# Rounding constants in two row groups, a later Silu, and earlier exponentials in an S4 and MLP block

## The chip, the cores and the metric

The kernel runs on one core of one Trainium2 chip. The core has five engines that run side by side: TensorE (PE) multiplies matrices into PSUM, VectorE (DVE) and ScalarE (ACT) work on elements, GpSimd (POOL) and SyncE (SP) here mostly issue transfers (DMA). Each works through its own instructions in order and waits on semaphores for the others. The metric is the device time of one execution in microseconds (us); less is better.

## The reference

The input is a sequence `x` of 2048 rows with 512 channels. A condition vector `c` is passed through Silu and multiplied by `w_mod`, which gives six rows of modulation: shift, scale and gate for each of two halves.

```python
mod = (_silu(c) @ w_mod).reshape(c.shape[0], 6, 1, -1)
h = _layernorm(x) * (1 + ca) + sa
x = x + ga * _A_ref(h, ...)      # S4: a long convolution along the sequence
h = _layernorm(x) * (1 + cb) + sb
x = x + gb * _B_ref(h, ...)      # dense 512 -> 1792, mish, dense 1792 -> 512
```

The convolution kernel of each channel is `K[d, l] = Re sum_n C[d,n] dB[d,n] exp(dt[d] A[d,n] l)` with 128 complex states `n` per channel and 2048 positions `l`; the reference convolves by FFT.

## The kernel before

The 512 channels are four blocks of 128; a block is worked in eight chunks of 16 channels, so there are 32 chunks `k`, with `b, c = divmod(k, 8)`. For each chunk the powers `exp(dt A l)` are made from a product of a fine and a coarse table, each of a magnitude (exponential) and an angle (sine and cosine).

*The parameters of block 0* come first and at the top of the program: `params(0, stage)` (lines 443 to 505) takes logarithm, exponential and an arc tangent (stages 1 and "atan", ScalarE) with VectorE's arithmetic between them, and leaves them split in `pk`. `load_s` (507) for block 0 spreads `pk` over partitions with matmuls (`psel`) and ScalarE copies (`s`). `coarse_mm` and `coarse` (533, 541) are the matmuls into `pco` and the exponentials of them into `co` and `cf`, four groups to a block.

*The angle of a chunk* is `s_ang` (554). It accumulates eight data matmuls into `pang` (two PSUM banks, one buffer), half with `ac`, half with `nac = -ac`. Between the two halves a large constant is added and subtracted again, which rounds what is there to a whole number, so that the second half leaves the negative fraction of a turn. The constant is made by matmuls of ones (`oneb`) against a column (`rnd`), 512 wide: in block 0 with all 128 rows and the constant divided by 128, four matmuls for a chunk; in blocks 1 to 3 with 32 rows and the constant divided by 32, the two banks in different row groups (rows 0 to 31 and 64 to 95), again four. `s_sin` (583) takes the absolute value and two sines from `pang` into `ec`, `s_mag` and `s_comb` (590, 599) multiply in the magnitudes on VectorE, `s_kgen` (610) contracts over the states on TensorE into `pkg`, and `s_ks`, `s_ka`, `s_tm` (622 to 640) bring the result into `gk`.

*The signal's side:* layer norm of the rows (`stats`, `norm_scales`, `norm`), a first transform (`ua`, with ScalarE's copies `us` and their stores to `ud` in DRAM), the modulation (`mod_load`, `mod_mm` and what follows; it reads `sc`, the output of Silu), then per step `gl`, `ubu`, `ug`, `ubk`, `prod`, `t1`, `yt`, `invb`, `z`. The shift's row passes through `srt`, `sra`, `srv` once, before the first `ubu`. After the convolution come a second layer norm and the MLP, from about 350 us on.

*Order.* V, A and T are wrappers (293) that keep the instructions of VectorE, ScalarE and TensorE in the order in which the program issues them. For the first chunks that order is written out by hand (lines 905 to 1106). For the rest `_plan` (57) makes it, a list scheduler: each operation has an engine, a cost in ns (`NS`), a due time (`LEAD` or `AT`, in chunks), what it depends on, and the PSUM banks that it takes from a ring of six and that another operation frees. An engine that is free takes the ready operation with the earliest due time; one whose banks are not yet free is passed over. A switch of ScalarE's table between sine (table "S") and exponential ("E") costs `SWITCH`, and once in "E" the planner holds sines back until the block's exponentials are done. `vt` (coarse matmuls, three banks each) and `va` (their exponentials) are numbered by group: `vt` and `va` 4 to 7 are those of block 1. `p0` to `p5` and `pa` are the stages of `params` for blocks 1 to 3, `ls` is `load_s`. An activation whose function is not in the loaded table set gets a load in front of it; `tables(...)` places one.

## Time and profile before

| | |
|---|---|
| median of 3 runs | 688.12 us (684.78 to 692.02) |
| the profiled execution | 687.09 us |
| its span, first to last instruction | 685.3 us |
| mean granted TensorE clock | 0.970 |
| TensorE busy | 626.3 us (91%) |
| VectorE busy | 475.4 us (69%) |
| ScalarE busy | 403.7 us (59%) |

The profile is of one execution. In a line of the order of time stand the start in us, the busy time in us, the engine, the line of the program, the operation, what it writes and reads with sizes, and how many instructions were merged (x); in brackets how long the engine was idle ahead of it, and what ended the wait. Nearly all instructions are issued through a helper, so their line is L301; they are told apart by their tiles. PEld is TensorE's loading of weights, which runs beside its matmuls. A line of waits has who waited for whom: us in total, times, and the longest.

### The profile page before, as it was taken

To read this page: it belongs to the slowest core of one execution; us is meant where nothing else is said; L and a number is where in the kernel's file an instruction comes from. 1 tells how busy PE (TensorE), PEld (TensorE's weight loads), DVE (VectorE), ACT (ScalarE), POOL (GpSimd) and SP (SyncE) were. 2 spreads that over 40 slices of the span, in tenths; PEclk is the share of its full clock that TensorE was granted. 3 is DMA by queue.
4 is the path that set the end of the run, shared out by engine and by line. 5 is a ranking of instruction groups with operands and counts; after the bars stand their busy time and mean duration, and the time that the engine had idled before them with its cause. 6 is when DMAs were issued, how large, how long until landed. Compare 5 with 4: busy or idle time off the path is not lost.

```text
span 685.3 us, 16585 instructions
## 1 busy us (share of the span) xinstructions
PE 626.3 (91%) x6740; PEld 506.1 (74%) x6746; DVE 475.4 (69%) x903; ACT 403.7 (59%) x707; POOL 101.5 (15%) x212
## 2 busy tenths in 40 slices
PE   0658878999989999999999999999999999999997
PEld 0424556778867777777875888789889898998996
DVE  5997974999689995997676799586337723653233
ACT  3478778877889769876653664453345334534231
POOL 2002705063406240000100000000000001000100
PEclk9979978799999999999999999999999999999999
DMA  9938978353457466555898987666334552273232
GB/s 253 213 151 247 239 182 218 101 144 76 103 161 188 128 182 174 153 146 160 248 269 235 316 284 241 229 176 200 116 93 141 167 154 94 93 222 116 93 93 62
DMA packets 108220, 117.55 MB, mean 172 GB/s; under 512 B 12904, under 2 KB 84976, under 8 KB 106992
## 3 DMA queue, kind: packets, MB, share of 16 engines
q1 hardware_dynamic: 93296, 85.62, 43.9%
q0 software_dynamic: 14464, 30.36, 15.6%
q8 instruction: 53, 0.87, 0.6%
q10 hardware_dynamic: 384, 0.52, 0.3%
q14 instruction: 23, 0.19, 0.1%
HBM read 81.85 MB, written 32.51 MB: 167 GB/s over the span
## 4 chain that ended last, share of the span: by engine, by line
PE 67%; DMA 12%; ACT 9%; DVE 7%; issue 3%; SPq 2%; ACTq 0%; DVEq 0%
PE pr L301 25%; PE pp L301 9%; PE pkg L301 7%; PE pang L301 6%; PE pub L301 5%; PE pib L301 4%; ACT ec L301 3%; PE pkb L301 3%; PE pt L301 2%; DMA xr<-in_A_u 2%; DMA wm<-in_w_mod 2%; DMA ud<-us 2%; PE pia L301 2%; DMA w1s<-in_B_w 2%; DMA w2s<-in_B_w 2%
## 5 line engine op out<-in xcount | busy, mean ns | idle before, releaser
L301 PE MATMUL pr<-hh,w 128*128 128x256 f32 (+1 forms) x420 | 78.2, 327 | 0.5 <-ACT hh L301 0.5
L301 ACT ACTIVATE ec<-pang 128x1024 f32<-128x1024 f32 x64 | 62.2, 1025 | 23.3 <-PE pang L301 23.3
L301 PEld LDWEIGHTS pr<-hh,w 128*128 128x128 f32 x420 | 66.6, 188 | 12.7 <-ACT hh L301 1.9
L301 DVE TENSOR_TENSOR mh<-x,pr 128x256 f32<-128x256 f32 x63 | 26.4, 419 | 65.2 <-PE pr L301 64.9
L301 PE MATMUL pp<-w,mah 128*128 128x512 f32 x224 | 70.5, 396 | 0.0
L301 PE MATMUL pr<-w,mah 128*128 128x512 f32 x224 | 70.0, 394 | 0.0
L301 DVE TENSOR_TENSOR ec<-ec,m 128x1024 f32<-128x1024 f32 x64 | 61.2, 957 | 9.9 <-ACT ec L301 7.8
L1259 POOL DMA_DIRECT2D w<-w2d x42 | 22.2, 529 | 300.9 <-PE pp L301 201.7
L301 ACT ACTIVATE mh<-mh,b 128x256 f32<-128x256 f32 x63 | 32.1, 510 | 52.4 <-DVE mh L301 52.1
L528 POOL DMA_DIRECT2D s<-pk x96 | 47.5, 501 | 61.9 <-PE pang L301 53.9
L301 ACT ACTIVATE mh<-pr,b 128x256 f32<-128x256 f32 (+1 forms) x35 | 19.4, 558 | 62.5 <-PE pr L301 62.5
L301 DVE TENSOR_TENSOR q<-pkb,ug 128x1024 f32<-128x1024 f32 x32 | 39.1, 1221 | 17.0 <-PE pkb L301 16.7
L301 DVE TENSOR_TENSOR mal<-mh,mah 128x512 fp32r<-128x512 f32 x56 | 38.5, 688 | 14.5 <-ACT mah L301 14.3
L301 DVE TENSOR_TENSOR m<-cf 128x1024 f32<-128x1024 f32 x32 | 39.0, 1218 | 13.7 <-ACT cf L301 13.7
L301 PE MATMUL pp<-w,mal 128*128 128x512 f32 x112 | 43.9, 392 | 0.0
L301 PE MATMUL pr<-w,mal 128*128 128x512 f32 x112 | 43.9, 392 | 0.0
L301 ACT ACTIVATE ug<-pub,gd 128x512 f32<-128x512 f32 x64 | 34.0, 590 | 14.9 <-PE pub L301 14.9
L301 PEld LDWEIGHTS pp<-w,mah 128*128 128x128 f32 x224 | 38.4, 189 | 4.9
L301 DVE TENSOR_TENSOR x<-x,pr 128x256 f32<-128x256 f32 x42 | 17.6, 420 | 34.4 <-PE pr L301 34.4
L301 PEld LDWEIGHTS pkg<-ec 128*32 128x32 f32 x2048 | 34.7, 115 | 8.0 <-issue 1.8
L526 POOL DMA_DIRECT2D s<-pk x48 | 23.8, 501 | 112.7 <-ACT ks L301 60.2
L301 PE MATMUL pkg<-ec 128*32 128x64 f32 x2048 | 40.1, 232 | 0.0
(172 smaller groups left out, 1421.6 us busy)
## 6 DMA issues: line engine op xcount, KB each, us to landing
w<-w2d POOLq DMA_DIRECT2D x42, 512.0 KB, 3.6
ud<-us SPq DMA_DIRECT2D x64, 128.0 KB, 2.7
gu<-ud SPq DMA_DIRECT2D x32, 256.0 KB, 3.0
zd<-z SPq DMA_DIRECT2D x32, 256.0 KB, 3.8
zt<-zd SPq DMA_DIRECT2D x32, 256.0 KB, 4.8
w2d<-w SPq DMA_DIRECT2D x14, 512.0 KB, 4.2
xf<-x2d SPq DMA_DIRECT2D x16, 256.0 KB, 5.0
x2d<-xp SPq DMA_DIRECT2D x14, 256.0 KB, 3.2
```

Source lines behind the costliest of these rows:

```text
L301: ins = f(*a, **kw)
L526: nc.gpsimd.dma_start(S3[b, i][q, :], pk[32 * i:32 * i + 32, 8 + k, :])
L528: nc.gpsimd.dma_start(S12[b, g][64 * e + 16 * k:64 * e + 16 * k + 16].rearrange("p h n -> p (h n)"), pk[d, k + 4 * e, :])
L1259: nc.gpsimd.dma_start(t, w2d[f])
```

## The change

Three edits. Silu of the condition moves from the head of ScalarE's program to just behind the arc tangent of block 0. The rounding in block 0 takes the form that blocks 1 to 3 have: 32 rows, the two banks in two row groups; for that the loop over the two halves of the data becomes the outer one. In the planner's tables the first coarse matmuls of block 1 (`v1`) get the due time -14 instead of -4.01, which holds for their exponentials too, and those matmuls depend on the sine of chunk 7 instead of chunk 8 (`- (b == 1)`); the exponentials still depend on the sine of chunk 8. The planner's cost of a `us` copy goes from 540 to 580.

```diff
-      "sc": 2600, "nr": 450, "ua": 1150, "us": 540, "we": 240, "na": 490, "lf": 60, "sr": 400}
+      "sc": 2600, "nr": 450, "ua": 1150, "us": 580, "we": 240, "na": 490, "lf": 60, "sr": 400}
...
-      "p0": -20.55, "p1": -7.87, "v1": -4.01, "v2": -4.01, "v3": -4.01, "vn": 1.22, "e1": 0, "e2": 0, "e3": 0,
+      "p0": -20.55, "p1": -7.87, "v1": -14, "v2": -4.01, "v3": -4.01, "vn": 1.22, "e1": 0, "e2": 0, "e3": 0,
...
-            op(("vt", 4 * b + n), "T", k + AT[f"v{b}"] + n * AT["vn"], [("ls", 2 * b, PART), ("sin", k + AT[f"e{b}"])], 3)
+            op(("vt", 4 * b + n), "T", k + AT[f"v{b}"] + n * AT["vn"], [("ls", 2 * b, PART), ("sin", k + AT[f"e{b}"] - (b == 1))], 3)
...
+    def rounding(p):
+        for z in range(2):
+            for e in range(2):
+                r = slice(64 * e, 64 * e + 32)
+                T.matmul(p[:, e, :], oneb[r].to_broadcast([32, P]), rnd[r, 2 + z:3 + z].to_broadcast([32, 512]),
+                         start=False, stop=False, skip_group_check=True)
+
...
-            for e in range(2):
-                for w in (ac, nac):
+            for w in (ac, nac):
+                for e in range(2):
                     for q in range(2):
...
-                    for z in range(2) if w is ac else ():
-                        T.matmul(p[:, e, :], oneb.to_broadcast([P, P]), rnd[:, z:z + 1].to_broadcast([P, 512]),
-                                 start=False, stop=False, skip_group_check=True)
+                if w is ac:
+                    rounding(p)
...
-            for z in range(2) if w is ah else ():
-                for e in range(2):
-                    r = slice(64 * e, 64 * e + 32)
-                    T.matmul(p[:, e, :], oneb[r].to_broadcast([32, P]), rnd[r, 2 + z:3 + z].to_broadcast([32, 512]),
-                             start=False, stop=False, skip_group_check=True)
+            if w is ah:
+                rounding(p)
...
-    act(sc, cT, AF.Silu)
     nc.sync.dma_start(hl, io["hl"])
...
     params(0, "atan")
+    act(sc, cT, AF.Silu)
     params(0, 2.6)
```

## The prediction

> **What bounds the kernel now.** I read the page first, then busy time by stage, then the waits of the engines up to 200 us, then the order of time in the three places that the diff touches. The first fence is the page's busy line and the busy time by stage (PE, PEld, DVE, ACT, POOL; then granted clock, DMA share, GB/s).

> ```profile
> PE 626.3 (91%) x6740; PEld 506.1 (74%) x6746; DVE 475.4 (69%) x903; ACT 403.7 (59%) x707; POOL 101.5 (15%) x212
> ...
> 0.00:25.00 25.00, 2.11 (x8) 1.43 (x8) 16.77 (x68) 6.31 (x10) 3.78 (x18) 1.00 0.99 245
> 25.00:50.00 25.00, 16.24 (x67) 10.90 (x68) 23.38 (x74) 18.31 (x31) 0.00 (x0) 0.80 0.64 178
> 50.00:75.00 25.00, 20.46 (x284) 10.25 (x281) 19.90 (x30) 20.99 (x37) 9.93 (x21) 0.86 0.83 224
> 100.00:125.00 25.00, 21.14 (x406) 16.07 (x400) 14.79 (x37) 18.43 (x32) 8.96 (x18) 0.77 0.79 216
> 125.00:150.00 25.00, 23.69 (x357) 17.97 (x357) 24.31 (x38) 21.41 (x38) 6.67 (x14) 0.93 0.38 104
> 150.00:175.00 25.00, 25.00 (x521) 20.27 (x523) 24.60 (x27) 16.96 (x32) 9.40 (x20) 1.00 0.36 90
> ```

> From 150 us on TensorE is busy in all of its 25.00 us at clock 1.00, with VectorE at 24.60 beside it: from there nothing that the diff touches can move the end, except by letting that stretch begin earlier. Before it TensorE is not full and its clock falls to 0.77. All three edits lie ahead of 135 us. So the question is how many microseconds each takes off the start of the full stretch.

> The waits of ScalarE up to 200 us name the two that the diff aims at:

> ```profile
> ACT ec L301 <- PE pang L301: 13.3, 10, 3.0
> ACT sc L301 <- DMA cT<-in_c: 10.3, 1, 10.3
> ```

> **Part 1, Silu behind the arc tangent.** The order of time at the start:

> ```profile
> 0.73 1.28 ACT L301 ACT_TABLE_LOAD   x1 [0.73 <-PEq L1521]
> ...
> 10.94 0.43 DVE L301 TENSOR_TENSOR raw<-raw 128x256 f32<-128x256 f32 x1
> 12.36 0.21 ACT L301 ACTIVATE sc<-cT 128x4 f32<-128x4 f32 x1 [10.34 <-DMA cT<-in_c]
> 12.58 1.28 ACT L301 ACT_TABLE_LOAD   x1
> ...
> 14.43 1.04 ACT L301 ACTIVATE early<-early 128x1024 fp32r<-128x1024 f32 x1
> 14.55 0.29 DVE L301 TENSOR_TENSOR raw<-raw 128x128 f32<-128x128 f32 x1 [3.19 <-ACT raw L301]
> ...
> 22.80 0.28 PEld L301 LDWEIGHTS psel<-pk,sel 32*128 32x128 f32 x1 [22.80 <-DVE pk L301]
> ...
> 24.62 0.99 ACT L301 CAST s<-psel 128x256 fp32r<-128x256 f32 x4 [5.82 <-PE psel L301]
> ...
> 25.66 0.69 DVE L301 BATCH_NORM_STATS2 bst<-xr 128x6 f32<-128x512 f32 x1
> ```

> Silu is ScalarE's first activation and waits 10.34 us for c, so the logarithm and its table load stand behind that load, and VectorE, done at 11.37, idles 3.19 us for them. With Silu moved, the load of the table runs at the start and the logarithm follows its input, which VectorE has written before 11.37. The next thing late is VectorE itself: it goes straight on. Gain 3.2 us for `pk`, the selections (22.80) and the statistics (25.66, no idle before). It can't be more, since VectorE has no second gap there: 25:50 holds 23.38 us of its work. It could be less if the constants that the negation at 14.43 reads, or the rows of x, came only just in time. The negation had no wait of its own, the statistics none either; I take 3.2, and 2 as the low end.

> Cost: Silu's own 0.21 us, and its table. The loads at 0.73 (for Silu) and at 12.58 show that Silu does not share the logarithm's set; whether it shares the arc tangent's no row shows, so nothing or one load of 1.28. Both fall into the 5.82 us in which ScalarE waits for the selections; only 4.3 us of them would have to go before it cost anything. c has landed by 12.36, so there is no new wait; `sc` is read first by the modulation matmuls near 48 us.

> **Part 2, rounding constants.** The old matmuls in a chunk of block 0 at full clock, the new form with its next group in a chunk of block 1, and an old pair at half clock in chunk 0:

> ```profile
> 80.69 0.38 PE L301 MATMUL pang<-rnd,oneb 128*128 128x512 bf16 x1
> ...
> 81.39 0.61 PE L301 MATMUL pang<-rnd,oneb 128*128 128x512 bf16 x2
> ...
> 135.88 0.61 PE L301 MATMUL pang<-rnd,oneb 32*128 32x512 bf16 x4
> 136.42 0.51 PE L301 MATMUL pang<-nah,s 64*128 64x256 f32 x4
> ...
> 28.37 1.08 PE L301 MATMUL pang<-rnd,oneb 128*128 128x512 bf16 x2
> ```

> A pair of the old form lasts 0.61 where one lasts 0.38, so each further one costs 0.23, and four 0.92. Four of the new form run two at a time: 0.61 for all, and 0.54 from their start to the next group's (135.88 to 136.42). The saving is 0.92 - 0.54 = 0.38 us a chunk at full clock, and about twice that, 0.75, at half clock (a pair takes 1.08 there). The reordering of the eight data matmuls changes nothing in their number or shape.

> [...]

> Only chunks for which ScalarE waits are worth anything:

> ```profile
> 31.71 0.99 ACT L301 CAST s<-psel 128x256 fp32r<-128x256 f32 x4 [1.74 <-PE psel L301]
> 43.56 1.94 ACT L301 ACTIVATE ec<-pang 128x1024 f32<-128x1024 f32 x2 [2.86 <-PE pang L301]
> 48.39 1.94 ACT L301 ACTIVATE ec<-pang 128x1024 f32<-128x1024 f32 x2 [1.85 <-PE pang L301]
> 94.30 1.94 ACT L301 ACTIVATE ec<-pang 128x1024 f32<-128x1024 f32 x2 [0.68 <-PE pang L301]
> 105.37 1.94 ACT L301 ACTIVATE ec<-pang 128x1024 f32<-128x1024 f32 x2 [3.04 <-PE pang L301]
> ```

> Chunk 0 stands in front of the second selections (1.74): one pair at half clock, one at full, 0.6. Chunk 1 at half clock: 0.75. Chunk 2, mixed: 0.55. Chunk 6 at full clock: 0.4. Chunk 7, mostly half: 0.7. Chunks 3 to 5 have no such wait in the timeline and count nothing. Sum 3.0 us, each inside its wait. Bounds: nothing if other work in front of TensorE fills the waits again, 4.1 if chunks 3 to 5 count too.

> **Part 3, the exponentials of block 1.** The stretch now, by ScalarE, VectorE and TensorE:

> ```profile
> 113.72 1.94 ACT L301 ACTIVATE ec<-pang 128x1024 f32<-128x1024 f32 x2
> ...
> 116.70 1.28 ACT L301 ACT_TABLE_LOAD   x1
> 118.00 1.09 ACT L301 ACTIVATE co<-pco 128x512 f32<-128x512 f32 x2
> ...
> 119.61 1.23 DVE L301 TENSOR_TENSOR m<-cf 128x1024 f32<-128x1024 f32 x1 [5.66 <-ACT cf L301]
> ...
> 118.65 1.92 PE L301 MATMUL pco<-mc,s 128*128 128x256 f32 x4 [3.22 <-ACT co L301]
> ...
> 130.57 1.28 ACT L301 ACT_TABLE_LOAD   x1
> ...
> 130.74 1.16 PE L301 MATMUL pkb<-mf,gk 128*128 128x128 f32 x8
> ```

> Two table loads there are and two there stay. Now the sine of chunk 9 (113.72) goes first, and VectorE idles 5.66 us until the first exponentials let `mag` of chunk 8 start at 119.61. With due time -14 the four coarse matmuls have the highest priority on TensorE, from the sine of chunk 7 on, and the exponentials the highest on ScalarE from the sine of chunk 8 on. So the sine of chunk 9, its 3.0 us, moves behind, and VectorE starts 3 to 4 us earlier. That is the gain, at most 4, if VectorE (24.31 of 25 in 125:150) sets the pace.

> Against it: the planner gives PSUM banks in a ring of six, in order. The first coarse matmul takes three of them ahead of `kgen` of chunk 6, whose two are then those that `tm` of chunk 5 must empty first; and `tm` has a late due time, so on ScalarE the table load, the first exponentials, `sra` and `p1` go before it. By the durations above (1.28, 1.6, and four copies or small ones of about half a microsecond) that is some 5 us in which TensorE has nothing, against 3.22 now; then `kgen` 6, `kgen` 7, `tm` 7 and the first `pkb` (130.74) follow later. Price 2 to 5 us on TensorE. The two nearly cancel. I take +0.5, between -4 and +5. The planner's cost of a `us` copy (540 to 580) changes no instruction, only which of two ready ones goes first; bounded within 1 us either way, taken as nothing.

> **Sum.** 3.2 + 3.0 - 0.5 = 5.7 us earlier at 135 us, and TensorE is full behind, so as much at the end. The profiled execution took 687.09 (span 685.3, 1.8 around it); the median of the runs is 688.12, 1.0 above. 687.1 - 5.7 = 681.4, and on the runs' footing 682.4.

> **The rivals.** *The head start is lost between 50 and 105 us, or part 2 is eaten by drains.* That stretch stores the transformed input with the DMA share at 0.83 (50:75), and ScalarE waits for the stores' tiles:

> ```profile
> ACT us L301 <- DMA ud<-us: 3.0, 5, 1.5
> 44.00:46.00 2.00, 0.45 (x3) 1.00 0.00 0
> ```

> [...] Against it: 3.0 us of waits in all, and the DMA stands idle before (share 0.00 at 44:46), so that an earlier start finds it free.

> *The exponentials pay as well:* VectorE's lead of 4 us arrives at the end, nothing is lost on TensorE: 682.4 - 4.5 = 678.

> *TensorE starves at the new switch, slower than before.* If everything behind `tm` 5 waits until the last exponentials (some 10 us instead of 5), TensorE idles 7 us more than now, the clock, 0.77 in 100:125 around the present gap, falls again and costs up to 5 more, and the full stretch begins 12 us later for this part: 682.4 + 11.5 = 694. It decides from the point at which `kgen` 6 comes behind the fourth coarse matmul and the first `pkb` over 6 us later, relative to the sine of chunk 8, than now. [...]

> *The exponentials don't move*, because no three banks are free when the sine of chunk 8 ends: then part 3 is nothing and the time is the forecast's.

> **How the numbers follow.** The forecast, 682.4 (own range 679 to 686), has 0.45, with the unmoved exponentials in it; the lost head start 0.2 (0.03 of it for the drains); the paying exponentials 0.2; the starved TensorE 0.15. A measurement of this kernel tells about 1% (6.9 us) from no change, so faster means below 681.2. Of the forecast's own chance a third lies there (0.15), all of the third case (0.2): 0.36 with rounding. Slower means above 695: two fifths of the last case and a little for the unnamed, 0.08. The rest, 0.56, is within. The range 675 to 691 leaves out the bad half of the last case, and the lower edge of the third.

> **What would show it.** No idle of VectorE near 11 us, `psel` near 19.6, Silu and a load inside ScalarE's wait for `psel`. Rounding rows 32*128 x4 in block 0, chunk 1 near 36 us with a wait of ScalarE near 2.1 instead of 2.86. `mag` of chunk 8 with less than 3 us idle before it. The store stage shifted by 5 to 6 us as a whole. Wrong it is if the first `us` copies shift and the last ones don't, or if TensorE's gap at the switch is over 8 us.

## The result, and the profile after

The kernel after took 682.95 us (median of 20 runs, 679.76 to 688.27), the kernel before 687.74 us in the runs beside them. The ratio is 0.9936, with a 95% interval of 0.9918 to 0.9953: 4.4 us less (3.2 to 5.6). One of the 20 runs of the kernel before took 1005.73 us, and the ratio, which is of the fast runs, leaves it out. The forecast was 682.4. The total was right; its terms were not all right, and the experiments below show which.

The profiled execution of after is the longest of its 20 runs (688.27 us), longer than that of before (687.09). Its span says nothing on the verdict. What it can show is where things stand, stage by stage. First the page's busy line and the busy time by stage (PE, PEld, DVE, ACT, POOL; then granted clock, DMA share, GB/s):

```profile
PE 631.9 (92%) x6746; PEld 507.0 (74%) x6746; DVE 475.4 (69%) x903; ACT 403.8 (59%) x707; POOL 101.3 (15%) x212
...
25.00:50.00 25.00, 16.21 (x76) 7.72 (x75) 23.27 (x72) 19.06 (x30) 0.00 (x0) 0.66 0.76 212
50.00:75.00 25.00, 20.54 (x308) 10.96 (x308) 21.06 (x28) 20.49 (x36) 12.49 (x26) 0.86 0.90 237
75.00:100.00 25.00, 22.22 (x360) 14.07 (x361) 19.71 (x33) 16.86 (x32) 3.30 (x7) 0.73 0.84 197
100.00:125.00 25.00, 22.28 (x400) 16.36 (x398) 17.91 (x45) 23.37 (x41) 8.96 (x18) 0.79 0.72 201
125.00:150.00 25.00, 22.03 (x395) 17.01 (x395) 24.18 (x27) 16.77 (x29) 15.76 (x32) 0.86 0.40 96
```

The row of 75 to 100 us in before, for comparison:

```profile
75.00:100.00 25.00, 19.87 (x355) 13.02 (x354) 19.38 (x27) 19.97 (x34) 5.88 (x12) 0.89 0.88 214
```

Three stages are worse than before in a column that the diff doesn't name, the granted clock: 0.66 against 0.80 in 25:50, 0.73 against 0.89 in 75:100, and 0.86 against 0.93 in 125:150. VectorE and ScalarE have not become busier on the whole (475.4 and 403.8 us, as before).

**The start.** ScalarE's order of time, and under it TensorE's first selection:

```profile
15.34 0.31 ACT L301 ACTIVATE raw<-raw 128x128 f32<-128x128 f32 x1 [2.77 <-DVE raw L301]
15.67 1.28 ACT L301 ACT_TABLE_LOAD   x1
16.97 0.21 ACT L301 ACTIVATE sc<-cT 128x4 f32<-128x4 f32 x1
21.47 0.99 ACT L301 CAST s<-psel 128x256 fp32r<-128x256 f32 x4 [4.29 <-PE psel L301]
```
```profile
19.65 2.11 PE L301 MATMUL psel<-pk,sel 32*128 32x384 f32 x8 [19.65 <-DVE pk L301]
```

The selections start at 19.65 instead of 22.80, 3.15 us earlier. Silu does need a load of its own (15.67), and load and Silu lie in ScalarE's wait for the selections, of which 4.29 us is still left.

**The chunks.** The waits of ScalarE up to 200 us for the angles, and for the stores of the first transform:

```profile
ACT ec L301 <- PE pang L301: 15.3, 11, 2.9
ACT us L301 <- DMA ud<-us: 0.4, 1, 0.4
```

The waits for `pang` were to shrink by some 3 us. They were 13.3 before and are 15.3 now. The wait for chunk 1, at half clock in both kernels, did shrink, from 2.86 to 2.40 (2.1 was foretold):

```profile
39.14 1.94 ACT L301 ACTIVATE ec<-pang 128x1024 f32<-128x1024 f32 x2 [2.40 <-PE pang L301]
```

The waits for the stores went from 3.0 to 0.4, and their copies start at 51.38 instead of 55.25, 3.9 us earlier, of which 3.15 were there at the selections:

```profile
51.38 0.57 ACT L301 COPY us<-pua 128x512 f32<-128x512 f32 x1
```

### The profile page after: what moved, and what is told of

Read it like the earlier page. It is cut to its first block, busy times and chain, and to the rows that moved or that the text cites. A ratio compares the mean times of both kernels' runs of the same rounds, so it can differ in the third digit from the quotient of the medians.

```text
span 686.5 us, 16596 instructions
## 1 busy us (share of the span) xinstructions
PE 631.9 (92%) x6746; PEld 507.0 (74%) x6746; DVE 475.4 (69%) x903; ACT 403.8 (59%) x707; POOL 101.3 (15%) x212
## 3 DMA queue, kind: packets, MB, share of 16 engines
q1 hardware_dynamic: 93296, 85.62, 44.1%
## 4 chain that ended last, share of the span: by engine, by line
PE 68%; DVE 12%; DMA 9%; ACT 7%; issue 3%; SPq 1%; DVEq 0%; ACTq 0%
PE pr L301 25%; PE pp L301 9%; PE pkg L301 7%; PE pang L301 6%; PE pub L301 5%; PE pib L301 4%; DMA xr<-in_A_u 3%; PE pkb L301 3%; ACT ec L301 2%; PE pt L301 2%; DVE raw L301 2%; DVE ec L301 2%; PE pia L301 2%; DMA w2s<-in_B_w 1%; DVE w L301 1%
## 5 line engine op out<-in xcount | busy, mean ns | idle before, releaser
L301 PE MATMUL pr<-hh,w 128*128 128x256 f32 (+1 forms) x420 | 78.2, 327 | 0.5 <-ACT hh L301 0.5
L301 ACT ACTIVATE ec<-pang 128x1024 f32<-128x1024 f32 x64 | 62.4, 1030 | 25.3 <-PE pang L301 25.3
L301 PEld LDWEIGHTS pr<-hh,w 128*128 128x128 f32 x420 | 66.6, 188 | 12.7 <-ACT hh L301 1.9
L301 DVE TENSOR_TENSOR mh<-x,pr 128x256 f32<-128x256 f32 x63 | 26.4, 419 | 65.2 <-PE pr L301 64.9
L301 PE MATMUL pp<-w,mah 128*128 128x512 f32 x224 | 71.3, 400 | 0.0
L301 PE MATMUL pr<-w,mah 128*128 128x512 f32 x224 | 70.4, 396 | 0.0
L301 DVE TENSOR_TENSOR ec<-ec,m 128x1024 f32<-128x1024 f32 x64 | 61.3, 957 | 9.8 <-ACT ec L301 4.8
L301 ACT ACTIVATE mh<-mh,b 128x256 f32<-128x256 f32 x63 | 32.1, 510 | 53.2 <-DVE mh L301 52.9
L301 ACT ACTIVATE mh<-pr,b 128x256 f32<-128x256 f32 (+1 forms) x35 | 19.4, 559 | 63.0 <-PE pr L301 63.0
L301 DVE TENSOR_TENSOR q<-pkb,ug 128x1024 f32<-128x1024 f32 x32 | 39.1, 1221 | 22.7 <-PE pkb L301 22.5
L301 DVE TENSOR_TENSOR mal<-mh,mah 128x512 fp32r<-128x512 f32 x56 | 38.6, 689 | 15.8 <-ACT mah L301 15.7
L301 DVE TENSOR_TENSOR m<-cf 128x1024 f32<-128x1024 f32 x32 | 39.0, 1218 | 10.2 <-ACT cf L301 10.2
L301 ACT ACTIVATE ug<-pub,gd 128x512 f32<-128x512 f32 x64 | 34.0, 590 | 20.4 <-PE pub L301 20.4
L301 PE MATMUL pr<-w,mal 128*128 128x512 f32 x112 | 44.3, 395 | 0.0
L301 PE MATMUL pp<-w,mal 128*128 128x512 f32 x112 | 44.2, 394 | 0.0
L301 PEld LDWEIGHTS pkg<-ec 128*32 128x32 f32 x2048 | 35.4, 117 | 11.1 <-ACT us L301 4.4
L301 PE MATMUL pkg<-ec 128*32 128x64 f32 x2048 | 40.8, 234 | 3.0 <-ACT us L301 1.9
L301 PEld LDWEIGHTS pp<-w,mah 128*128 128x128 f32 x224 | 38.9, 191 | 5.1
L301 DVE TENSOR_TENSOR x<-x,pr 128x256 f32<-128x256 f32 x42 | 17.6, 419 | 34.3 <-PE pr L301 34.3
```

The lines of the kernel that those rows point to most:

```text
L301: ins = f(*a, **kw)
```

## The experiments

**Silu alone.** The edit to before:

```diff
-    act(sc, cT, AF.Silu)
...
     params(0, "atan")
+    act(sc, cT, AF.Silu)
```

> The kernel before with Silu alone moved. Forecast's theory: VectorE's gap of 3.19 us near 11 us closes, everything behind it moves 3.2 us earlier as a whole, and the end with it: ratio 0.9953, 684.5 us beside 687.7. Rival (the stores between 50 and 105 us take the head start): selections 3.2 us earlier, last us copy less than 1 us earlier, ratio 0.999 to 1.000.

Measured: 685.41 us, ratio 0.9950 (0.9921 to 0.9979), so 3.4 us less (1.4 to 5.4). This agrees with the term of the sum, 3.2; that the median lies so near it is chance, with this interval. In its trace the last copies `us` come at 95.29 instead of 98.15 and the sine of chunk 9 at 110.75 instead of 113.72, about 2.9 us earlier, so the stores do not take the head start.

**Rounding alone.** The edit is the change's `rounding` and the exchanged loops, nothing else.

> The kernel before with the 32-row rounding alone. The prediction's price of 3.0 us on ScalarE's waits: ratio 0.9956, 684.7 us. Rival, from the changed kernel's profile: a chunk at full clock takes 1.94 us from its first start to its last end against 2.10 before, and at half clock 3.34 against 3.82, so the saving is 0.16 and 0.48 and about 1.3 us on the same five waits: ratio 0.998, 686.4 us.

Measured: ratio 1.0014 (0.9989 to 1.0039). The forecast's 3.0 us lie outside the interval. Either the chunks aren't shorter, or their length is worth nothing, or something gives it back.

**The planner's cost of a `us` copy alone.**

```diff
-      ... "ua": 1150, "us": 540, "we": 240, ...
+      ... "ua": 1150, "us": 580, "we": 240, ...
```

> The kernel before with the planner's cost of a us copy at 580 alone; the planner then sets the sine of chunk 4 and of chunk 5 and the angles of chunk 4 ahead of some copies, and nothing behind chunk 6 changes. Prediction: within 1 us, ratio 0.9985 to 1.0015. Rival: the order of the store stage is worth more than that, ratio below 0.9975 or above 1.0025.

Measured: ratio 0.9983 (0.9957 to 1.0010), 1.2 us less, with no change at all inside the interval. This is a fourth edit beside the three that the description of the change counts.

**The due time of block 1's exponentials alone.**

```diff
-      ... "v1": -4.01, ...
+      ... "v1": -14, ...
...
-            ... ("sin", k + AT[f"e{b}"])], 3)
+            ... ("sin", k + AT[f"e{b}"] - (b == 1))], 3)
```

> The kernel before with the early exponentials of block 1 alone (due time -14, dependence on the sine of chunk 7). Prediction's net: +0.5 us, ratio 1.0007, between -4 and +5. Rival a (the exponentials pay): 4 us less, ratio 0.994. Rival b, from the changed kernel's profile: the sine of chunk 10 comes earlier by 2.5 us more than the one of chunk 8, but prod of step 0 stands behind comb of chunk 10 in VectorE's order and comes 3.8 us later than before, so that TensorE runs dry near 137 us and its clock halves again: 2 to 4 us more, ratio 1.003 to 1.006.

Measured: ratio 0.9992 (0.9966 to 1.0019). The four edits alone give -3.4, +1.0, -1.2 and -0.6 us, together -4.2; the whole change gave -4.4. Each of the four is uncertain by some 2 us, so no large interplay is to be seen, and the question is why the rounding is worth nothing.

**Is the length of the angle chunks on the path at all?** Two runs double and remove the old form's work.

```diff
-                    for z in range(2) if w is ac else ():
+                    for z in (0, 1, 0, 1) if w is ac else ():
```
```diff
-                    for z in range(2) if w is ac else ():
+                    for z in ():
```

> The kernel before with each rounding of block 0 made twice in the old form (eight 128-row matmuls a chunk instead of four; the second pair of constants rounds what is rounded already). A chunk grows by 0.92 us at full clock and 1.75 at half, 2.4 times what the prediction let it save. If ScalarE's waits pass a chunk's length on to the end as the prediction priced it (3.0 us for 0.38 and 0.75): 7 us more, ratio 1.010. If TensorE's fuller windows bring the clock back sooner and pay for it, or other work hides it: ratio 0.998 to 1.004.

> The kernel before with the rounding of block 0 left out altogether, so that the angles of block 0 cancel to nothing and its output is not the reference's; everything else runs as before. A chunk shrinks by 0.92 us at full clock and 1.75 at half, without any change of the tiling mode. If a chunk's length is on the path and only the mode changes ate the gain of the 32-row form: 5 to 7 us less, ratio 0.990 to 0.993. If the length is not what counts (the time comes back in the clock or in the next wait): ratio 0.997 to 1.001.

Measured: with the rounding twice the ratio is 1.0078 (1.0047 to 1.0109), 5.4 us more; without it 0.9918 (0.9888 to 0.9948), 5.6 us less. The first lies between its two expectations, the second at the first of its two. The length is on the path. And these traces give the bare price of each form. The order of time on TensorE, a chunk at full clock: without rounding, with the old form (before), with the new one (after). The last line of each is the next work, so that the distance from the first line is what the chunk takes:

```profile
61.52 1.22 PE L301 MATMUL pang<-early,s 128*128 128x256 f32 x8
62.67 0.27 PE L301 MATMUL pkg<-bdk,ks 64*64 64x64 f32 x1
```
```profile
80.12 0.50 PE L301 MATMUL pang<-early,s 128*128 128x256 f32 x2
...
82.16 0.27 PE L301 MATMUL pkg<-bdk,ks 64*64 64x64 f32 x1
```
```profile
60.33 0.74 PE L301 MATMUL pang<-early,s 128*128 128x256 f32 x4
60.99 0.61 PE L301 MATMUL pang<-rnd,oneb 32*128 32x512 bf16 x4
61.53 0.74 PE L301 MATMUL pang<-early,s 128*128 128x256 f32 x4
62.19 0.27 PE L301 MATMUL pkg<-bdk,ks 64*64 64x64 f32 x1
```

1.15 us, 2.04 and 1.86. The old rounding costs 0.89, the new 0.71: a saving of 0.18 where the prediction had 0.38. The old price (forecast 0.92) was right, and so was the 0.54 of the group of four (60.99 to 61.53). What was missed stands beside the group: each of the two groups of data takes 0.66 to the next start, together 1.32, where eight in a row take 1.15. That is 0.17 for the two changes of the tiling, beside 0.08 inside the group (0.54 against 2 x 0.23). At half clock, without rounding and in after:

```profile
42.98 2.07 PE L301 MATMUL pang<-early,s 128*128 128x256 f32 x8 [2.03 <-ACT ec L301]
44.98 1.08 PE L301 MATMUL pmodr<-wm,sc 128*32 128x512 f32 x4
```
```profile
41.13 1.23 PE L301 MATMUL pang<-early,s 128*128 128x256 f32 x4 [2.03 <-ACT ec L301]
42.29 1.03 PE L301 MATMUL pang<-rnd,oneb 32*128 32x512 bf16 x4
43.25 1.22 PE L301 MATMUL pang<-early,s 128*128 128x256 f32 x4
44.41 1.08 PE L301 MATMUL pmodr<-wm,sc 128*32 128x512 f32 x4
```

2.00 and 3.28; the old form, in the kernel after with the old rounding (next), takes 3.84 from its first start to its last end (36.98 to 40.82) where after takes 3.34 by the same ends (41.13 to 44.47):

```profile
36.98 0.79 PE L301 MATMUL pang<-early,s 128*128 128x256 f32 x2 [5.63 <-ACT ec L301]
...
39.83 0.99 PE L301 MATMUL pang<-early,s 128*128 128x256 f32 x2
```

The saving there is 0.50, not 0.75. With 0.18 and 0.50 in the prediction's own five chunks (half and half in chunks 0 and 2, half clock in 1, nearly so in 7, full in 6) the sum is 0.34 + 0.50 + 0.34 + 0.18 + 0.45 = 1.8 us, not 3.0. By the same reckoning the old form (0.89 and 1.76 a chunk) makes 6.9 us on these chunks, of which the two runs above found 5.4 and 5.6: about four fifths of a chunk's length reach the end. The interval of rounding alone ends at 0.8 us of gain, so that 1.8 and four fifths of it are outside, and something more is gone.

**The change with the old rounding.** After, with block 0's loops and rounding as before.

```diff
-            for w in (ac, nac):
-                for e in range(2):
+            for e in range(2):
+                for w in (ac, nac):
...
-                if w is ac:
-                    rounding(p)
+                    for z in range(2) if w is ac else ():
+                        T.matmul(p[:, e, :], oneb.to_broadcast([P, P]), rnd[:, z:z + 1].to_broadcast([P, 512]),
+                                 start=False, stop=False, skip_group_check=True)
```

> The changed kernel with the old rounding (128 rows, four matmuls, banks in turn). By the prediction's price it loses 3.0 us against the changed kernel: ratio to the kernel before 0.998. By the run with the rounding alone (1.0014, 0.9989 to 1.0039) the rounding is worth nothing here either: ratio 0.991 to 0.995, as the changed kernel's 0.9936 or a little below it.

Measured: 0.9932 (0.9907 to 0.9957), the same as after. In its place, too, no gain of the rounding edit is to be seen, though the two intervals together leave room for some 2 us.

**More rows, and the order alone.** Before with 64 rows a group (`rounding_64`), the order of the loops without the new form (`order_only`), and after with 64 rows. The diff shows the rows; the constants get a third pair, divided by 64.

```diff
-                r = slice(64 * e, 64 * e + 32)          # rounding_64, after_rounding_64: block 0 only
-                T.matmul(p[:, e, :], oneb[r].to_broadcast([32, P]), rnd[r, 2 + z:3 + z].to_broadcast([32, 512]),
+                r = slice(64 * e, 64 * e + 64)
+                T.matmul(p[:, e, :], oneb[r].to_broadcast([64, P]), rnd[r, 4 + z:5 + z].to_broadcast([64, 512]),
```
```diff
+            for w in (ac, nac):                         # order_only
+                for e in range(2):
                     for q in range(2):
...
+                for e in range(2) if w is ac else ():
+                    for z in range(2):
+                        T.matmul(p[:, e, :], oneb.to_broadcast([P, P]), rnd[:, z:z + 1].to_broadcast([P, 512]),
```

> Only the rounding of block 0, in two row groups of 64 rows instead of 32: the two groups still run side by side and the tiling still changes twice a chunk, but all 128 rows of the array work, as in the form of before. Theory that the changes of tiling alone took the gain: the chunk is as long as with 32 rows (1.94 us at full clock, 3.34 at half), the time at half clock is what it was with 32 rows (49.7 us on the mean of its runs, against 43.4 of the kernel before), and the ratio is 0.999 to 1.003. Theory that the clock goes by how many rows work: the same chunk length, but half clock near 43 us, and a ratio of 0.996 to 0.998. If the 64-row groups don't run side by side, the chunk is longer than 2.1 us at full clock and the ratio is above 1.003.

> Only the order of block 0's matmuls: the first operand's data matmuls of both halves, then the four rounding matmuls in the form of before (128 rows), then the second operand's. No change of tiling. If the order costs nothing, the chunk is 2.10 us at full clock and 3.83 at half as before, and the ratio is 0.998 to 1.002. If the order is what took the gain of the rounding edit, the chunk is 0.2 us or more longer and the ratio is 1.003 to 1.005.

> The kernel after, with 64 rows a group in block 0's rounding instead of 32. Theory that the clock goes by the rows that work: half clock falls from 44.1 us (mean of the runs of after) towards 38.3 (after with the old rounding), and the ratio is 0.989 to 0.991, better than after. Theory that it goes by the length of the work, or that only the changes of tiling count: 0.992 to 0.995, as after.

Measured: 64 rows alone 1.0002 (0.9983 to 1.0020), the order alone 1.0008 (0.9983 to 1.0033), after with 64 rows 0.9906 (0.9880 to 0.9933). In the trace of the order alone a chunk takes 2.05 us (64.45 to 66.50), where before has 2.04. A chunk with 64 rows is as long as with 32, 1.87 us:

```profile
64.22 0.74 PE L301 MATMUL pang<-early,s 128*128 128x256 f32 x4
64.89 0.61 PE L301 MATMUL pang<-rnd,oneb 64*128 64x512 bf16 x4
...
66.09 0.27 PE L301 MATMUL pkg<-bdk,ks 64*64 64x64 f32 x1
```

So the order costs a chunk nothing, and 64 rows cost it what 32 do. Both forms change the tiling. The theory that the clock goes by the rows that work got one answer against it and one for it: alone, 64 rows gave neither the ratio nor the clock that it foretold (0.996 to 0.998, 43 us at half clock; the table below has 46.6), but after with 64 rows came out where it said, at 0.9906. That run has six executions, and its interval holds 0.9932 as well, so this stays open.

**Where the shorter chunks' lead goes.** In the trace of before with 64 rows the first copies `us` start at 54.20 instead of 55.25, 1.05 us earlier. At the sine of chunk 9 nothing is left of it (113.67 against 113.72, and 113.67 with 32 rows too). The rows of the copies in before, then of the copies and the sine with 64 rows:

```profile
55.25 0.57 ACT L301 COPY us<-pua 128x512 f32<-128x512 f32 x1
```
```profile
54.20 0.57 ACT L301 COPY us<-pua 128x512 f32<-128x512 f32 x1
...
113.67 1.94 ACT L301 ACTIVATE ec<-pang 128x1024 f32<-128x1024 f32 x2
```

The busy time of most of the stretch between, before and then with 64 rows, differs in the clock (0.88 and 0.80):

```profile
50.00:100.00 50.00, 40.33 (x630) 23.27 (x634) 39.27 (x57) 40.96 (x71) 15.81 (x32) 0.88 0.86 219
```
```profile
50.00:100.00 50.00, 41.93 (x605) 22.71 (x605) 38.08 (x55) 38.37 (x68) 15.81 (x32) 0.80 0.86 217
```

Up to the sine of chunk 9 before has 27.3 us at half clock, and the traces with 32 and with 64 rows have 34.1 each. One execution can be chance. The mean clock of every run is known, though, and the granted clock takes two values in these traces, full (1.00) and half (0.50), so the time at half clock is 2 x (1 - clock) x span. Means over the runs, with their standard errors:

| kernel | runs | us at half clock |
|---|---|---|
| before, beside the next four | 35 | 43.4 ± 0.8 |
| rounding alone (32 rows) | 12 | 49.7 ± 2.7 |
| Silu alone | 12 | 44.1 ± 1.1 |
| early exponentials alone | 12 | 42.0 ± 1.4 |
| cost of a `us` copy alone | 12 | 39.1 ± 1.3 |
| before, beside the next four | 23 | 42.5 ± 0.9 |
| order alone | 12 | 42.9 ± 1.2 |
| rounding alone (64 rows) | 12 | 46.6 ± 1.4 |
| after with 64 rows | 6 | 39.7 ± 3.0 |
| Silu and the cost of a `us` copy | 6 | 37.7 ± 1.5 |
| before, beside the next four | 29 | 42.8 ± 0.8 |
| no rounding | 12 | 45.6 ± 1.9 |
| rounding twice | 7 | 39.0 ± 0.6 |
| after with the old rounding | 11 | 38.3 ± 1.1 |
| after with `tm` earlier | 12 | 45.3 ± 2.9 |
| after, on its own | 20 | 44.1 ± 2.0 |

With less for TensorE to do the clock stays low longer: by 6.3 ± 2.8, 4.1 ± 1.7 and 5.8 ± 2.3 us (32 rows, 64 rows, after against after with the old rounding), and by 2.8 ± 2.1 with no rounding; with the rounding doubled it is 3.8 ± 1.0 less. By medians instead of means the first three are 4.0, 1.4 and 3.3. After with 64 rows, with six runs, shows little (1.4 ± 3.2). But the work is not all: the cost of a `us` copy, which changes only an order, takes 4.3 ± 1.6 off.

What such time goes with can be read from the runs of one and the same kernel: over 233 runs of all kernels the span grows by 0.20 us for each us more at half clock (a correlation). By that estimate the mean of the three, 5.4 us, costs 1.1 us. Of 1.8 us 0.7 stay, a tenth of a per cent, which none of these intervals can tell from nothing.

**The order at the switch.** After, with the copies `tm` of block 0 earlier:

```diff
-        op(("tm", k), "A", lead("tm", k), [("ka", k)], frees=[("kgen", k)])
+        op(("tm", k), "A", lead("tm", k) - 14 * (k < 8), [("ka", k)], frees=[("kgen", k)])
```

> The changed kernel with the due time of tm in block 0 fourteen chunks earlier, so that on ScalarE tm of chunk 5 goes ahead of the table load and prod of step 0 ahead of comb of chunk 10 on VectorE. If the early exponentials lose on TensorE what they gain on VectorE because kgen 6 and prod 0 stand behind, as the run with them alone shows (prod 0 8.2 us later, sine of chunk 10 2.6 us earlier): 2 to 4 us less than the changed kernel, ratio to the kernel before 0.988 to 0.991. If that order costs nothing: 0.9936.

Measured: 0.9972 (0.9946 to 0.9998), neither of the two that were expected, and worse than after by the medians. The first product still comes late (136.07 in its trace, 136.55 in after), so `tm` 5 is not what holds it. The edit also moves copies in the store stage, so that this run can't say more.

**Without rounding and without the early exponentials.** Before with the two edits that are left:

```diff
-      ... "us": 540, ...
+      ... "us": 580, ...
...
-    act(sc, cT, AF.Silu)
...
     params(0, "atan")
+    act(sc, cT, AF.Silu)
```

> Silu behind the arc tangent and the planner's cost of a us copy at 580; rounding and due time of the exponentials as before. If the two small gains add up and the early exponentials are worth nothing in place: 0.995 x 0.998 = 0.993, as after. If the exponentials pay only together with the head start: 0.995 to 0.997, worse than after. If they cost something in place: below 0.992.

Measured: 683.47 us, ratio 0.9926 (0.9900 to 0.9952). Two edits do what the whole change does, as far as these intervals tell. In its trace the head start is there at three places: the first copy `us` at 52.21 (3.04 earlier), the sine of chunk 9 at 110.27 (3.45), the MLP's matmuls at 370.72 against 373.63 in before (2.91). The rows of before with the two edits, then the last one's in before:

```profile
52.21 0.57 ACT L301 COPY us<-pua 128x512 f32<-128x512 f32 x1
...
110.27 1.94 ACT L301 ACTIVATE ec<-pang 128x1024 f32<-128x1024 f32 x2
...
370.72 9.27 PE L301 MATMUL pr<-hh,w 128*128 128x512 f32 x36 [0.54 <-ACT hh L301]
```
```profile
373.63 9.27 PE L301 MATMUL pr<-hh,w 128*128 128x512 f32 x36 [0.54 <-ACT hh L301]
```

The last place can't be read from one trace: in that of Silu alone the lead is 2.97 us at the sine of chunk 9, and yet the MLP's matmuls start at 374.67, 1.0 us later than in before. That execution took 687.15 us, 1.7 more than the median of its kernel.

## Why the prediction was right or wrong

**What bounds the kernel: right.** The lead of Silu is there before and behind the stores between 50 and 105 us (3.15 us at the selections, 2.97 at the sine of chunk 9 in its own trace), so they don't hold it. That it reaches the end is shown by the runs, 3.4 us (1.4 to 5.4), not by single traces: with the two edits 3.45 us at 110 us become 2.91 at the MLP, with Silu alone 2.97 become none.

**Part 1, Silu: right in size and place.** The prediction had 3.2, and measured are 3.15 at the selections and 3.4 (1.4 to 5.4) in time. The load that no row could settle is there, 1.28 us, and hidden, as bounded.

**Part 2, rounding: wrong.** The step that failed is "The saving is 0.92 - 0.54 = 0.38 us a chunk at full clock, and about twice that, 0.75, at half clock". Measured: 0.18 and 0.50. The price of the old form held (0.92 foretold, 0.89 measured), and so did the 0.54 of the packed group, which was read from a chunk of block 1, from the group's start to the next group's. What the neighbouring groups lose at the changes of tiling, 0.17 us a chunk, lies outside that interval and so is not in the 0.38. With the 0.08 inside the group the two changes cost 0.25 us a chunk at full clock, 0.125 each. The prediction also has a rival in which drains eat part 2, with a chance of 0.03. No run shows a drain; in its place the traces show this loss.

That makes 1.8 us of 3.0. The first three chunks gave about what these prices say (1.05 us at the first `us` copy in the trace with 64 rows, 0.34 + 0.50 + 0.34 = 1.2 by prices). It is gone by the sine of chunk 9, in traces with 6.8 us more at half clock up to there. So for this term, and only for it, the head start was lost in the stretch that the first rival named; the clock is the likely reason, and the stores are not, since Silu's lead passes them.

**Part 3, the exponentials: right as a sum within the noise, and the mechanism of its price wrong.** Order-of-time lines on VectorE for `mag` of chunk 8 and the first product, with the late exponentials (before with the two edits), then with the early ones (after with the old rounding); the two kernels differ in nothing else:

```profile
116.16 1.23 DVE L301 TENSOR_TENSOR m<-cf 128x1024 f32<-128x1024 f32 x1 [5.67 <-ACT cf L301]
...
129.34 1.22 DVE L301 TENSOR_TENSOR q<-pkb,ug 128x1024 f32<-128x1024 f32 x1
```
```profile
112.65 1.23 DVE L301 TENSOR_TENSOR m<-cf 128x1024 f32<-128x1024 f32 x1 [2.14 <-ACT cf L301]
...
137.38 1.22 DVE L301 TENSOR_TENSOR q<-pkb,ug 128x1024 f32<-128x1024 f32 x1
```

VectorE starts 3.5 us earlier and idles 2.14 us instead of 5.67, as foretold (3 to 4, under 3). On TensorE the first `pkb` comes 3.3 us later, inside the 2 to 5 that were foretold:

```profile
127.65 1.16 PE L301 MATMUL pkb<-mf,gk 128*128 128x128 f32 x8
```
```profile
130.94 1.16 PE L301 MATMUL pkb<-mf,gk 128*128 128x128 f32 x8
```

But the reason given for it is not borne out: at the new switch TensorE has no gap of some 5 us, its longest there is 1.72 instead of 3.22. It did other work first, and the rival in which it starves falls. The first product on VectorE comes 8.0 us later, because VectorE, busy without a gap, does the work of two more chunks ahead of it. TensorE waits for that later. Its rows with the early exponentials:

```profile
110.56 0.50 PE L301 MATMUL pco<-mc,s 128*128 128x512 f32 x1 [1.72 <-DVE q L301]
...
132.65 1.16 PE L301 MATMUL pkg<-ec 128*32 128x64 f32 x64 [0.56 <-DVE ec L301]
...
139.47 0.71 PE L301 MATMUL pt<-ident,ug 128*128 128x128 f32 x4 [1.22 <-DVE ug L301]
```

From 100 to 150 us TensorE is busy for 45.19 us with the late exponentials and for 45.25 with the early ones, at clock 0.88 and 0.87. VectorE's lead did not become a lead of TensorE, which is full behind, and the two kernels take the same time, 0.9926 and 0.9932 of before. This is one trace of each. Whether the early exponentials cost a microsecond or give one stays open: alone they measured 0.6 us less with an interval from 2.3 less to 1.3 more.

**The cost of a `us` copy: taken as nothing within 1 us, measured 1.2 less (3.0 less to 0.7 more).** Its runs were at half clock for 39.1 ± 1.3 us against 43.4; at 0.20 us for each that is 0.9 us. This is consistent with the gain; neither is shown.

**The sum.** Foretold 3.2 + 3.0 - 0.5 + 0 = 5.7, from the profiled run of before with 1.0 added for the median; measured 3.4 - 1.0 + 0.6 + 1.2 = 4.2 by single edits and 4.4 together. By single edits the rounding brought 4.0 us less than foretold, the two edits that were put at -0.5 together 2.3 more, and Silu 0.2 more; 1.5 us are left of these, or 1.3 against the whole change. The two errors went against each other, and that the total came so near is in part luck. The 2.3 is within the noise of the two runs that it comes from. The limit of 1%, or 6.9 us, for what can be told from no change was too wide: with 20 runs of each kernel 4.4 us can.

Of the signs named, those of the start and of `mag` were seen. The first and the last `us` copies both shifted (51.38 against 55.25, 93.63 against 98.15); the first moved by 3.9 us and not by 5 to 6, since the rounding's part of it was 0.7 and not 1.9.

## What to carry to other kernels

Price a replaced form by the whole block it stands in, from the start of the block to the next work behind it, and look at the neighbours' rows: of the 0.25 us that two changes of tiling cost a chunk here, 0.17 are not in the row of the new instructions. A shorter program for an engine need not be a shorter time in the same measure: here chunks shorter by 1.8 us in sum went with 6.3 us (32 rows) and 4.1 us (64 rows) more at half clock, and with ratios of 1.0014 and 1.0002. Compare the clock over all runs before saying where a gain went. Of several edits made at once, test also the ones that were put at zero, and the kernel without the doubtful ones: here the kernel with two of the four edits is as fast as the one with all.

## What had not been expected of the hardware

In one trace a wait of 1.52 us is followed by 10.20 us at half clock, and in another the same wait, which falls elsewhere in the rhythm of 3.41 us, by none. In the run with 64 rows TensorE waits 1.52 us for ScalarE, and then works 10.20 us, three windows, without a gap at clock 0.50, with VectorE nearly full beside it (TensorE is the first busy number, VectorE the third). The wait lies whole in the window that ends at 135.15, of which TensorE was busy for 1.87 us:

```profile
134.83 0.80 PE L301 MATMUL pt<-ident,ug 128*128 128x128 f32 x4 [1.52 <-ACT ug L301]
```
```profile
131.74:135.15 3.41, 1.87 (x70) 1.67 (x70) 3.38 (x4) 3.27 (x6) 0.00 (x0) 1.00 0.28 82
135.20:145.40 10.20, 10.20 (x77) 7.59 (x79) 9.76 (x14) 5.16 (x9) 3.95 (x8) 0.50 0.10 21
```

With 32 rows alone the same instruction waits as long, but a window ends at 134.59, inside the wait. The two windows that share it are busy for 2.10 and 3.17 us, and the clock stays full:

```profile
134.83 0.63 PE L301 MATMUL pt<-ident,ug 128*128 128x128 f32 x4 [1.53 <-ACT ug L301]
```
```profile
131.18:134.59 3.41, 2.10 (x72) 1.76 (x70) 3.38 (x4) 3.41 (x6) 0.00 (x0) 1.00 0.28 82
134.59:138.00 3.41, 3.17 (x53) 2.26 (x54) 3.38 (x5) 2.02 (x5) 0.00 (x0) 1.00 0.00 0
135.20:145.40 10.20, 10.20 (x192) 7.93 (x191) 9.82 (x15) 7.55 (x12) 3.95 (x8) 1.00 0.38 102
```

In before the clock falls at 118.47, at the end of the gap of 3.22 us, and it also falls beside shorter waits: at 70.68, just behind a wait of 2.01 us, and at 87.75, at the end of one of 2.02. The windows that end there were 11%, 41% and 47% busy.

From one profiled run to the next the time at half clock goes from 34 us (before with the two edits, clock 0.975) to 61 (after, 0.955), and the runs of one kernel differ by 1.4 to 2.6 us in span (standard deviation): a term of a microsecond can't be read off two traces.

The number of rows that a row group spans made no difference to a packed pair of matmuls: 0.61 us for four with 32 rows and with 64.
